# An attention and expert kernel on one core: routing steps on VectorE alone, decayed keys and x on GpSimd, one product for both halves, and first weights every second unit

## The chip, the cores and the metric

The kernel runs on one NeuronCore of a Trainium2 chip. The core has five engines with instruction streams of their own: PE (TensorE, matrix products), DVE (VectorE, elementwise work and small reductions), ACT (ScalarE, activation functions and copies), POOL (GpSimd, elementwise work and indirect transfers) and SP (SyncE, transfers). They share the on-chip memory SBUF; PE writes its results to PSUM, which has eight banks of 128 x 512 numbers of four bytes. The metric is the device time of the core in microseconds, the median of several executions. The results must agree with the reference below.

## The reference

Two stages. The first is a gated linear attention, given as a recurrence over the sequence: batch 4, heads 8, length S = 768, head dimension D = 40. The second is a mixture of experts over the resulting rows: 4 x 768 = 3072 tokens of 320 numbers, eight experts, two of them for each token.

```python
for t in range(S):
    m_new = np.maximum(f_gate[:, :, t] + m, i_gate[:, :, t])
    f_stab = np.exp(f_gate[:, :, t] + m - m_new)
    i_stab = np.exp(i_gate[:, :, t] - m_new)
    m = m_new
    C = f_stab * C + i_stab * einsum('bhd,bhe->bhde', vt, kt)
    n = f_stab * n + i_stab * kt
    h_tilde = einsum('bhde,bhe->bhd', C, qt)
    denom = np.maximum(np.abs(einsum('bhd,bhd->bh', n, qt)), 1.0)
    y[:, :, t] = sigmoid(o_gate[:, :, t]) * h_tilde / denom
...
x = y.transpose(0, 2, 1, 3).reshape(3072, 320)
logits = x @ w_gate + np.log1p(np.exp(x @ w_noise)) * noise
top2, top2_w = two largest of 8, softmax over the two
for e in range(8):
    for k in range(2):
        mask = top2[:, k] == e
        h = np.maximum(x[mask] @ w1[e], 0.0)          # 320 -> 1024
        out[mask] += top2_w[mask, k, None] * (h @ w2[e])   # 1024 -> 320
```

## The kernel before, in words

**Attention by units.** The sequence is cut into 12 chunks of L = 64 positions, and the four batches into two pairs. A unit is one chunk of one pair, 128 tokens; there are NU = 24, units 0 to 11 for the first pair and 12 to 23 for the second. The loop `while i < NU` works on three units at once. For unit i it does the state update `c_part` (decayed keys KD times values, by PE; ScalarE copies the state into the next unit's values), the outputs `o_part` (products P times values, into the one bank "o") and `f_part` on DVE, which forms the denominator `dn`, the quotient `tm` and x, `xr = tm * sigmoid(gate)`. For unit i+1 it makes the decayed keys (`k_part`) and the products (`p_part`: scores times weights W, for both halves p = 0, 1 of the partitions, which are the two batches of a pair). For unit i+2 it makes the gate exponents `e_part` (PE, then Exp on ScalarE into W) and the scores `s_part`. It transposes x of unit i-1 (`t_part`) and multiplies the transposed x of unit i-2 by the gate's weights (`l_part`), which gives the router's logits. In the first chunk of a pair there is nothing before it to add, and the last chunk makes no update.

**Routing by groups.** Four units make a group; when the logits of a group are there, `route` starts a generator `g_part`. Its steps are given out between the instructions of the unit loop by `fill(n)`: `f1` of them at the unit's start and one after each of the first denominator steps, `f2` at its end, as the table `RATE` says. A step that must wait for ScalarE or PE yields "wait" and ends the filling. The steps are: softplus of the noise logits (`na`, `t1`, `co`, `ln`, with Exp and Ln issued on ScalarE by `act`), noise and sum (`nl`), the two largest (`mx`, `mi`), a mask `m` and its running sum `base`; then PE is asked for ranks (a request in the list `want`, served by `r_part`); from the ranks follow each token's slot `ix`, its parts `ai` and `bi`, and the one-hot tiles OA (128 x 448, then multiplied by a sign column) and OB (two of 128 x 512). The list `bursts` then asks PE for eight matmuls of these tiles (`b_part`), whose result is added to the slot table TBL. There is one OA and one OB for all groups. For groups below PG = 4 the softplus steps and the sign product run on POOL, for the others on DVE.

**Experts.** When the first four groups are in the table, four tiles of the first expert's tokens are gathered (`gather(0, 0)`) from the rows that `keep_rows` has written to HBM. From then on the eight experts run one after another: `mm1` (320 to 1024), `mm2` (1024 to 320) and an indirect add into the output. All matrix products there are made of high and low parts in three products.

**What sets the order.** Every engine runs its instructions in the order in which the program issues them; nothing is rescheduled. So an instruction that waits holds back all that stands behind it on its engine, transfers that the engine issues among them. PSUM is given out as eight named banks: one "e", four for scores ("s0" and "s1", two each), one "st" for the state, one "xt" for transposes, logits, ranks and bursts, one "o". SP loads the units' inputs three units ahead, and from unit 6 on pieces of the first expert's first weights, one a unit; `split_w1` then makes the high part on ScalarE and the low part (`w1l`) on POOL, one piece a unit from unit 8 to 13. POOL also writes x to HBM (`keep_rows`) up to unit 11, moves the gates of the units ahead (`gate_move`, every second unit up to 13), and from unit 14 on makes xr itself (XAT = 14). The order within a unit is, for DVE: `k_part(i + 1)`, routing steps, the denominators with routing steps between them, tm and xr, `p_part(i + 1)`, routing steps.

Of the kernel before, what the change touches and what calls it, by code (L numbers as in the profile page):

```python
# [18 lines left out]
L = 64  # L19
# [14 lines left out]

PG = 4
# [3 lines left out]
RATE = ((10, (1, 3)), (14, (3, 4)), (18, (4, 6)), (NU, (6, 9)))  # L39

XAT = 14
# [7 lines left out]
XV = 13  # L49
GC = 2  # L50
# [3 lines left out]
W1LD, W1AT, W2AT = 6, 8, 14  # L54
# [10 lines left out]
def build(ctx, tc, qk, vk, fi, noise, wgn, w1, w2, cst, ce, out):  # L65
# [203 lines left out]
    SP.dma_start(cs[:, C_TRI:], cst[:, C_TRI:])  # L269
    SP.dma_start(wgt, wgn)  # L270
    SP.dma_start(nzt, noise)
# [16 lines left out]
    for j in range(2):  # L288
        for p in range(2):
            psum.tile([128, 512], F32, name=f"s{p}", bufs=2)  # L290
# [29 lines left out]
    def s_room(u):  # L320
        SQ[u] = [psum.tile([128, 512], F32, name=f"s{p}", bufs=2).rearrange("p (h t) -> p h t", h=H) for p in range(2)]

    def s_part(u):
        q = QK[u % 4]
        if whole(u):

            for p in range(2):
                r = qrow[p]
                T.matmul(SQ[u][p][r], ident[r, r], q[r, 0], start=True, stop=True)
        for h in range(H):  # L330
            for p in range(2):
                r = qrow[p]
                T.matmul(SQ[u][p][half[p], h, :], q[r, 1, h, :], q[r, 0, h, :], start=True, stop=True)  # L333
# [4 lines left out]
    def k_part(u):  # L338
        if u % NCH < NCH - 1:
            KD[u] = wk.tile([128, 2, H, D], F32, name="kd")  # L340
            V.tensor_mul(KD[u], VKS[u % 4][:, :, 328:648].rearrange("p x (h d) -> p x h d", h=H),
                         W[u][:, :, :, L - 1:L].to_broadcast([128, 2, H, D]))

    def p_part(u):
        w = W[u]
        PP[u] = [wk.tile([128, H, L], F32, name=f"p{p}") for p in range(2)]
        for p in range(2):
            n = kr(u, p) if whole(u) else half[p]
            V.tensor_mul(PP[u][p][n], SQ[u][p][n], w[n, p])  # L349
# [14 lines left out]
    def o_part(u):  # L364
        for h in range(H):
            for p in range(2):
                n = kr(u, p)
                T.matmul(OQ[u][half[p], h, :], PP[u][p][n, h, :], VK[u % 4][p][n, h * 41:h * 41 + 41], start=True, stop=True)  # L368

    def f_part(u, step):  # L370
# [11 lines left out]
        (P if u >= XAT else V).tensor_mul(XR[u], tm.rearrange("p h d -> p (h d)"), SG[u % 4])  # L382
# [24 lines left out]
    def l_part(i):  # L407

        t = XTB if i < NU else psum.tile([128, 512], F32, name="e")
# [17 lines left out]
    def b_part(t):  # L427

        b = bursts.pop(0) if bursts else None
# [48 lines left out]
    def g_part(g):  # L478
# [7 lines left out]
        Q = P if g < PG else V  # L486
        na = sm("na", [128, nb, NE])
        if Q is P:
            P.tensor_scalar(na, s, 0.0, 2.0, op0=OP.max, op1=OP.mult)
            P.tensor_sub(na, s, na)  # L490
        else:
            V.scalar_tensor_tensor(na, s, -1.0, s, op0=OP.mult, op1=OP.min)
# [6 lines left out]
        Q.tensor_scalar(t1, ue, 1.0, None, op0=OP.add)  # L499
# [8 lines left out]
        Q.tensor_mul(co, co, na)  # L508
# [3 lines left out]
        Q.tensor_sub(ln, ln, co)  # L512
        yield
        if Q is P:
            P.tensor_scalar(na, s, 0.0, None, op0=OP.max)
            P.tensor_add(ln, ln, na)
        else:
            V.scalar_tensor_tensor(ln, s, 0.0, ln, op0=OP.max, op1=OP.add)
        yield
        Q.tensor_mul(ln, ln, nzt[:, u0:u0 + nb, :])  # L520
        yield
        nl = sm("nl", [128, nb, NE])
        Q.tensor_add(nl, ln, lg[:, :, 0:8])
# [36 lines left out]
        asked = [m[:, :, 1:], base[:, :, 0:nb], base[:, :, nb], rk, False]  # L560
# [43 lines left out]
        while busy and not (done[0] >= u0):  # L604
# [6 lines left out]
        (P if g < PG else V).tensor_mul(OA[:, 0:n], OA[:, 0:n].bitcast(F32),  # L611
                                        cs[:, C_SGN + 2 * u0:C_SGN + 2 * u0 + n, None].to_broadcast([128, n, C]))
# [5 lines left out]
        bursts.append((OBS(n), OAS(n)))  # L618
# [60 lines left out]
    turn = dict(h=0, x=0, y=0)  # L679

    def bank(use):

        n = dict(h=("s0", "s1", "e"), x=("s0", "s1"), y=("st", "o"))[use]
        turn[use] += 1
        name = n[turn[use] % len(n)]
        return psum.tile([128, 512], F32, name=name, bufs=2 if name in ("s0", "s1") else 1)
# [66 lines left out]
    begun = 0  # L753
    clear = zeros()
    pre1 = split_w1(P)
    i = 0
    while i < NU:
        f1, f2 = at(RATE, i)
        while sent:
# [3 lines left out]
        if i:  # L763
            keep_rows(i - 1)
        if i % 2 == 0 and i and i // 2 + 2 < 2 * GB:
            gate_move(i // 2 + 2, (P, P) if i < XV else (SP, SP))

        if W1LD <= i < W1LD + 6:
            piece_w1(0, 512 * ((i - W1LD) // 3), (i - W1LD) % 3)
        if W2AT <= i < W2AT + 4:  # L770
            early_w2(2 * (i - W2AT), 2)
        if i == 3:
            constants()
# [4 lines left out]
        if i + 1 < NU:  # L778
            k_part(i + 1)
        if i + 2 == NU:  # L780
            p_part(i + 1)
        if i == 0:
            sig_part(0)
        if i == 6:
            V.tensor_copy(tri, cs[:, C_TRI:C_TRI + 128])
            V.tensor_copy(ones, cs[:, C_ONE:C_ONE + 128])
        fill(f1)
# [8 lines left out]
        if i + 2 < NU:  # L796
            p_part(i + 1)
# [29 lines left out]
        if W1AT <= i < W1AT + 6:  # L827
# [341 lines left out]
```

## Time and profile before

| | us |
|---|---|
| median of 3 runs | 596.63 |
| lowest and highest run | 592.9, 598.4 |
| the profiled execution, its own time | 597.4 |
| its span from the first to the last instruction | 595.5 |
| start and units 0 to 2 | 0 to 40.5 |
| units 3 to 5 | 40.5 to 54.5 |
| units 6 to 21 | 54.5 to 161.5 |
| units 22, 23, last logits | 161.5 to 175.1 |
| experts | 175.1 to 595.5 |

A unit is counted here from the start of its outputs on PE (`o_part`, line 368) to the next one's. Rows of the trace give the start and the length in microseconds, the engine, the line, the operation, the output and inputs with their shape, and in brackets the idle time of the engine just before, with what ended it. A row in which several instructions are taken together ends in their count (x8). Granted clock 1.00 means that PE ran at full speed, 0.50 at half.

### The profile page before, as it was taken

How to read it: one execution, taken by the hardware profiler on the slowest of the kernel's cores; microseconds unless marked ns; L12 is line 12 of the kernel's file. 1: busy time of each engine (PE TensorE's matmuls, PEld its weight loads, DVE VectorE, ACT ScalarE, POOL GpSimd, SP SyncE). 2: the span in 40 equal slices, each digit the busy share in tenths (PEclk: the TensorE clock that was granted, in tenths of full speed). 3: DMA queues.
4: the chain of work that ended last, by engine and by line, in shares of the span. 5: the costliest groups of instructions: out<-in, count | busy, mean ns of one | idle time of the engine just before them, and what ended most of it. 6: DMA issues, size and time to landing. Idle time of an engine off the chain costs nothing.

```text
span 595.5 us, 13323 instructions
## 1 busy us (share of the span) xinstructions
PE 556.7 (93%) x5158; PEld 509.3 (86%) x5158; DVE 353.6 (59%) x958; ACT 255.5 (43%) x621; POOL 229.7 (39%) x308
## 2 busy tenths in 40 slices
PE   7679879999966999999999999999999999999995
PEld 3568767798865889899899989989999998998995
DVE  8589775877867627665466366456546635644611
ACT  6556745575642225452253155135225415423500
POOL 8133445424322446604623441470452245142043
PEclk9789867697877999999999999999999999999998
DMA  5868875568313965626443533642544253232024
GB/s 141 200 179 218 230 148 149 158 176 218 84 58 101 334 192 73 183 89 145 69 122 76 92 85 98 148 93 88 136 68 119 55 132 80 89 42 32 2 28 48
DMA packets 40918, 71.10 MB, mean 119 GB/s; under 512 B 8746, under 2 KB 30207, under 8 KB 40849
## 3 DMA queue, kind: packets, MB, share of 16 engines
q1 hardware_dynamic: 29488, 51.20, 30.0%
q0 software_dynamic: 11360, 18.98, 18.4%
q8 instruction: 43, 0.70, 0.5%
q14 instruction: 27, 0.21, 0.1%
HBM read 52.73 MB, written 17.73 MB: 118 GB/s over the span
## 4 chain that ended last, share of the span: by engine, by line
PE 76%; DVE 9%; issue 4%; POOL 3%; DMA 3%; ACT 1%; SPq 1%; another core or an unknown queue 1%; POOLq 0%; DVEq 0%
PE s L877 21%; PE e L877 10%; PE st L896 5%; PE st L895 5%; PE st L897 5%; PE o L896 4%; PE o L895 4%; PE o L897 4%; PE s L746 3%; DMA re<-hl 2%; PE s L333 2%; PE o L368 2%; PE st L359 1%; DVE p L349 1%; PE e L308 1%
## 5 line engine op out<-in xcount | busy, mean ns | idle before, releaser
L921 POOL DMA_INDIRECT y_out<-y,tok x56 | 87.3, 1558 | 217.5 <-DVE y L911 216.7
L877 PE MATMUL s<-xh,w1h 128*128 128x512 f32 (+1 forms) x255 | 76.8, 357 | 0.9 <-DVE xh L750 0.9
L748 ACT ACTIVATE xh<-s 128x384 fp32r<-128x384 f32 (+1 forms) x56 | 25.6, 470 | 105.5 <-PE s L746 105.1
L883 DVE SCALAR_TENSOR_TENSOR hlo<-s,hh 128x512 fp32r<-128x512 f32 (+1 forms) x85 | 47.4, 559 | 37.4 <-ACT hh L882 33.5
L716 POOL DMA_INDIRECT xg<-rows,tok x56 | 57.3, 1022 | 26.1 <-issue 12.2
L877 PE MATMUL s<-xh,w1l 128*128 128x512 f32 (+1 forms) x255 | 62.2, 353 | 0.0
L882 ACT ACTIVATE hh<-s 128x512 fp32r<-128x512 f32 (+1 forms) x85 | 41.9, 492 | 45.0 <-PE s L877 35.2
L895 PE MATMUL st<-w2h,hh 128*128 128x320 f32 x184 | 58.2, 316 | 0.0
L896 PE MATMUL st<-w2l,hh 128*128 128x320 f32 x184 | 57.3, 311 | 0.0
L897 PE MATMUL st<-w2h,hlo 128*128 128x320 f32 x184 | 56.9, 309 | 0.0
L895 PE MATMUL o<-w2h,hh 128*128 128x320 f32 x168 | 53.2, 317 | 0.0
L896 PE MATMUL o<-w2l,hh 128*128 128x320 f32 x168 | 52.3, 312 | 0.0
L897 PE MATMUL o<-w2h,hlo 128*128 128x320 f32 x168 | 52.0, 310 | 0.0
L877 PEld LDWEIGHTS s<-xh,w1h 128*128 128x128 f32 x255 | 46.3, 190 | 6.3 <-ACT xh L748 1.0
L877 PEld LDWEIGHTS s<-xh,w1l 128*128 128x128 f32 x255 | 44.8, 189 | 5.3
L877 PE MATMUL s<-xl,w1h 128*128 128x512 f32 (+1 forms) x170 | 46.2, 353 | 0.5 <-DVE xl L749 0.5
L333 PE MATMUL s<-qk 64*64 64x64 f32 x768 | 41.1, 255 | 0.2
L333 PEld LDWEIGHTS s<-qk 64*64 64x64 f32 x768 | 35.6, 164 | 3.6 <-issue 1.4
L877 PE MATMUL e<-xh,w1h 128*128 128x320 f32 (+1 forms) x129 | 38.5, 352 | 0.0
L749 DVE TENSOR_TENSOR xl<-s,xh 128x256 fp32r<-128x256 f32 (+1 forms) x56 | 22.6, 404 | 24.0 <-ACT xh L748 23.8
L368 PE MATMUL o<-vk,p 104*64 104x41 f32 (+2 forms) x768 | 31.5, 244 | 5.6 <-DVE t L499 3.9
L311 ACT ACTIVATE w<-e 128x512 f32<-128x512 f32 x46 | 27.6, 601 | 20.3 <-PE e L308 20.3
(212 smaller groups left out, 1350.8 us busy)
## 6 DMA issues: line engine op xcount, KB each, us to landing
vk<-vk_in SPq DMA_DIRECT2D x48, 242.0 KB
raw<-w_in SPq DMA_DIRECT2D x7, 1280.0 KB
qk<-qk_in SPq DMA_DIRECT2D x48, 160.0 KB
raw<-w_in SPq DMA_DIRECT2D x7, 1024.0 KB
y_out<-zrow SPq DMA_DIRECT2D x15, 320.0 KB
raw<-w_in SPq DMA_DIRECT2D x18, 256.0 KB
rows<-xr POOLq DMA_DIRECT2D x12, 160.0 KB
rows<-xr SPq DMA_DIRECT2D x12, 160.0 KB
```

Of the source, the lines that this page charges most:

```text
L311: A.activation(W[u][:, p].rearrange("p h t -> p (h t)"), ps, AF.Exp)
L333: T.matmul(SQ[u][p][half[p], h, :], q[r, 1, h, :], q[r, 0, h, :], start=True, stop=True)
L368: T.matmul(OQ[u][half[p], h, :], PP[u][p][n, h, :], VK[u % 4][p][n, h * 41:h * 41 + 41], start=True, stop=True)
L716: P.indirect_dma_start(out=XG[0:rows_of(t), t], out_offset=None, in_=XD[0:n], in_offset=bass.IndirectOffsetOnAxis(ap=token(e, t), axis=0), ...
L748: A.activation(XH[:, :, c], ps[:, :, 0:n], AF.Copy)
L877: T.matmul(ps[:, 0:n], l, r, start=i == 0, stop=i == len(ops) - 1)
L882: A.activation(HH[:, f, c], ps[:, 0:m], AF.Relu)
L883: V.scalar_tensor_tensor(HLO[:, f, c], ps[:, 0:m], 0.0, HH[:, f, c].bitcast(F32), op0=OP.max, op1=OP.subtract)
L895: T.matmul(ps, HH[:, j, c], W2H[:, j], start=j == 0, stop=False)
L896: T.matmul(ps, HH[:, j, c], W2L[:, j], start=False, stop=False)
L897: T.matmul(ps, HLO[:, j, c], W2H[:, j], start=False, stop=j == 7)
L921: st = P.indirect_dma_start(out=out, out_offset=bass.IndirectOffsetOnAxis(ap=token(e, t), axis=0), in_=y[0:n], in_offset=None, compute_op= ...
```

## The change

The names of new and moved parts, in the order of the diff:

- **k_part and xr:** both products run on POOL, the decayed keys from unit 2 on (KP), xr always. `k_part(i + 1)` is issued directly behind `keep_rows(i - 1)`, ahead of `gate_move`.
- **p_part:** the scores of both halves are one tile of two banks, and one instruction of 128 x 1024 makes the products, other than in the first chunk of a pair. It is issued at the unit's start, ahead of `fill(f1)` and of the denominators of unit i, not behind them.
- **Routing:** all steps on DVE, some of them in a shorter form; a new RATE; requests for ranks and bursts carry the unit from which PE may serve them: the next unit for groups 0 to 2, the same one for the later groups.
- **Weights and constants:** pieces of first weights are loaded and split every second unit, the low part on DVE; the early second weights are loaded from unit 19 on in place of 14; a part of the constants is loaded at unit 3, the noise at unit 4, and `constants()` runs at unit 6.
- **Experts:** the four first gathers are two at unit 22 and two at unit 23; last logits use the bank "st"; the banks for expert products are halves of the two-bank tile.

On DVE, in unit 10, the part of group 0's routing that makes the one-hot tiles stands in these rows before (dn, tm and xr belong to unit 10, p and kd to unit 11):

```order
L599 TENSOR_SCALAR ai_1362<-ix_1344 128x8
L602 SCALAR_TENSOR_TENSOR bi_1364<-ai_1362,ix_1344 128x8
L608 TENSOR_TENSOR oa<-cs,ai_1362 128x448
L373 TENSOR_SCALAR dn<-o 128x8
L615 TENSOR_TENSOR ob<-cs,bi_1364 128x512
L375 SCALAR_TENSOR_TENSOR dn<-o,dn 128x8
L615 TENSOR_TENSOR ob<-cs,bi_1364 128x512
L377 RECIPROCAL dn<-dn 128x8
L381 TENSOR_TENSOR tm<-o,dn 128x320
L382 TENSOR_TENSOR xr<-tm,vk_104 128x320
L349 TENSOR_TENSOR p_1420<-s_1239,w 104x512
L349 TENSOR_TENSOR p_1421<-s_1240,w 128x512
```

The same place on DVE after the change:

```order
L587 TENSOR_SCALAR ai_1310<-ix_1305 128x8
L342 TENSOR_TENSOR p<-s,w 128x1024
L590 SCALAR_TENSOR_TENSOR bi_1325<-ai_1310,ix_1305 128x8
L596 TENSOR_TENSOR oa<-cs,ai_1310 128x448
L599 TENSOR_TENSOR oa<-oa,cs 128x448
L603 TENSOR_TENSOR ob<-cs,bi_1325 128x512 x2
L370 TENSOR_SCALAR dn<-o 128x8
L372 SCALAR_TENSOR_TENSOR dn<-o,dn 128x8
L484 SCALAR_TENSOR_TENSOR na_1375<-lg 128x32
L374 RECIPROCAL dn<-dn 128x8
L378 TENSOR_TENSOR tm<-o,dn 128x320
```

The product p has moved ahead of the one-hot tiles and the denominators, the sign product stands in the row behind oa, and all four one-hot rows are ahead of the first dn.

On PE, at the end of group 0's routing, before the change, the burst (xt from oa and ob) stands in unit 10, behind that unit's logits (xt from wgt):

```order
L308 MATMUL e<-re_90,le_92 128x512
L413 MATMUL xt<-wgt,xts 128x16 x3
L433 MATMUL xt<-oa,ob 128x56 x8
L393 MATMUL xt<-cs,xr 128x128 x3
L308 MATMUL e<-re_90,le_92 128x512
```

After the change, from unit 10's state update (st from vk and kd) on:

```order
L356 MATMUL st<-vk_104,kd 40x41 x16
L365 MATMUL o<-vk_104,p 64x41 x16
L303 MATMUL e<-re_90,le_92 128x512
L410 MATMUL xt<-wgt,xts 128x16 x3
L390 MATMUL xt<-cs,xr 128x128 x3
L303 MATMUL e<-re_90,le_92 128x512
L328 MATMUL s<-qk_98 64x64 x16
L365 MATMUL o<-vk_105,p 64x41 x16
L303 MATMUL e<-re_90,le_92 128x512
L410 MATMUL xt<-wgt,xts 128x16 x3
L430 MATMUL xt<-oa,ob 128x56 x8
```

The burst has moved behind the outputs and logits of unit 11; unit 11, the last chunk of its pair, makes no update (st) ahead of its outputs.

On POOL, around units 9 and 10, before (rows<-xr is `keep_rows`, le and re are the gates of units ahead):

```order
L385 DMA rows<-xr 128x320
L145 TENSOR_TENSOR w1l<-raw_113,w1h 128x512
L830 MEMSET xg 128x336
L385 DMA rows<-xr 128x320
L220 DMA le_93<-hl 32x2x64
L222 DMA re_91<-hl 1x16x128 x2
L611 TENSOR_TENSOR oa<-oa,cs 128x448
L443 TENSOR_TENSOR tbl<-tbl,share 128x56
L489 TENSOR_SCALAR na_1467<-lg 128x32
```

And after:

```order
L382 DMA rows<-xr 128x320
L336 TENSOR_TENSOR kd<-vk_104,w 128x640
L379 TENSOR_TENSOR xr<-tm,vk_103 128x320
L832 MEMSET xg 128x336
L382 DMA rows<-xr 128x320
L218 DMA le_93<-hl 32x2x64
L220 DMA re_91<-hl 1x16x128 x2
L379 TENSOR_TENSOR xr<-tm,vk_104 128x320
```

In place of the weights' low part, the sign product and the softplus, POOL's queue now holds kd and xr of each unit, kd ahead of the gate transfers and xr behind them; unit 11 needs no kd.

The diff, cut to its core:

```diff
-PG = 4
-RATE = ((10, (1, 3)), (14, (3, 4)), (18, (4, 6)), (NU, (6, 9)))
-XAT = 14
+RATE = ((16, (3, 5)), (NU, (5, 8)))
+KP = 2
-W1LD, W1AT, W2AT = 6, 8, 14
+W1LD, W1AT, W2AT = 6, 8, 19
...
     def s_room(u):
-        SQ[u] = [psum.tile([128, 512], F32, name=f"s{p}", bufs=2).rearrange("p (h t) -> p h t", h=H) for p in range(2)]
+        SQ[u] = psum.tile([128, 2, 512], F32, name="s", bufs=2).rearrange("p x (h t) -> p x h t", h=H)
...
-            V.tensor_mul(KD[u], VKS[u % 4][:, :, 328:648].rearrange("p x (h d) -> p x h d", h=H),
+            (P if u >= KP else V).tensor_mul(KD[u], VKS[u % 4][:, :, 328:648].rearrange("p x (h d) -> p x h d", h=H),
...
     def p_part(u):
+        PP[u] = wk.tile([128, 2, H, L], F32, name="p")
+        if whole(u):
+            V.tensor_mul(PP[u], SQ[u], W[u])
...
-        (P if u >= XAT else V).tensor_mul(XR[u], tm.rearrange("p h d -> p (h d)"), SG[u % 4])
+        P.tensor_mul(XR[u], tm.rearrange("p h d -> p (h d)"), SG[u % 4])
...
-        w = want.pop(0) if want else None
+        w = want.pop(0) if want and want[0][5] <= unit[0] else None
...
-        b = bursts.pop(0) if bursts else None
+        b = bursts.pop(0) if bursts and bursts[0][2] <= unit[0] else None
...
-        asked = [m[:, :, 1:], base[:, :, 0:nb], base[:, :, nb], rk, False]
+        asked = [m[:, :, 1:], base[:, :, 0:nb], base[:, :, nb], rk, False, unit[0] + (g < 3)]
...
-        (P if g < PG else V).tensor_mul(OA[:, 0:n], OA[:, 0:n].bitcast(F32),
+        V.tensor_mul(OA[:, 0:n], OA[:, 0:n].bitcast(F32),
...
-        bursts.append((OBS(n), OAS(n)))
+        bursts.append((OBS(n), OAS(n), unit[0] + (g < 3)))
...
-    pre1 = split_w1(P)
+    pre1 = split_w1(V)
...
         if i:
             keep_rows(i - 1)
+        if i + 1 < NU:
+            k_part(i + 1)
...
-        if W1LD <= i < W1LD + 6:
-            piece_w1(0, 512 * ((i - W1LD) // 3), (i - W1LD) % 3)
+        if W1LD <= i < W1LD + 12 and i % 2 == 0:
...
-            gather(0, 0)
+            begun = 1
+        if begun and late < len(tiles(0, 0)):
+            n = 2 if i + 1 < NU else 4
+            gather(0, 0, tiles(0, 0)[late:late + n])
+            late += n
             begun = 2
...
+        if i + 1 < NU:
+            p_part(i + 1)
         fill(f1)
...
         f_part(i, fill if i + 2 < NU else (lambda: None))
-        if i + 2 < NU:
-            p_part(i + 1)
```

More of the change, by code (lines that the diff above doesn't have):

```diff
@@ L288, in build @@
     for j in range(2):
-        for p in range(2):
-            psum.tile([128, 512], F32, name=f"s{p}", bufs=2)
+        psum.tile([128, 2, 512], F32, name="s", bufs=2)
     psum.tile([128, 512], F32, name="st")
@@ L507, in g_part @@
         yield
-        Q.tensor_mul(co, co, na)
+        V.tensor_mul(co, co, na)
         while acts:
@@ L750, in transpose_x @@
         V.tensor_sub(XH[0:64, 2, c], ps[64:128, 2, 0:n], XH[64:128, 2, c].bitcast(F32))
-    begun = 0
+    begun = late = 0
+    unit = [0]
     clear = zeros()
-    pre1 = split_w1(P)
+    pre1 = split_w1(V)
     i = 0
@@ L758, in build @@
         f1, f2 = at(RATE, i)
+        unit[0] = i
         while sent:
```

65 lines of the change are left out of this document (30 added, 35 removed).

## The prediction

> **What bounds the kernel now.** I read a table of stages first, then TensorE's rows with an idle time in front, then DVE and POOL grouped by line, then the rows around single stalls.
>
> ```profile
> span 595.5 us, 13323 instructions
> ...
> 40.50:54.50 14.00, 14.00 (x344) 12.55 (x338) 12.01 (x32) 11.23 (x27) 3.23 (x6) 1.00 0.63 166
> 54.50:161.50 107.00, 97.45 (x1792) 86.44 (x1788) 80.89 (x270) 65.91 (x169) 46.51 (x84) 0.80 0.66 171
> 161.50:175.10 13.60, 9.07 (x108) 8.38 (x105) 7.79 (x29) 5.45 (x15) 5.56 (x6) 0.72 0.25 76
> 175.10:595.50 420.40, 406.60 (x2493) 381.50 (x2492) 222.49 (x558) 149.98 (x371) 154.19 (x172) 0.99 0.43 100
> ```
>
> The stage rows give window, length, then busy time of PE, PEld, DVE, ACT and POOL, the granted clock, the DMA share and GB/s. From 175.1 us the experts run with PE busy 97% at clock 0.99; nothing in the diff shortens their matmuls. What can move is the attention, three stages of it. Units 3 to 5 (40.5 to 54.5) show what a unit costs undisturbed: PE never idle, full clock, 14.00/3 = 4.67 us. Units 6 to 21 (54.5 to 161.5) do the same work with routing mixed in and take 107.0 us for 16 units, 6.69 each.
>
> Of these 107.0 us PE is idle 107.0 - 97.45 = 9.6. Its need at full clock is 16 x 4.67 = 74.7 plus four bursts at 1.18 (row at 156.71 below) = 4.7, so 79.4. The other 97.45 - 79.4 = 18.0 us are matmuls slowed by a lower clock. A state update in undisturbed units (49.18), the idle places, and the stretches at half clock:
>
> ```profile
> 49.18 0.82 PE L359 MATMUL st<-vk,kd 104*40 104x41 f32 x32
> ...
> 63.17 0.68 PE L308 MATMUL e<-re,le 98*128 98x512 f32 x1 [0.91 <-ACT w L311]
> 82.85 1.91 PE L433 MATMUL xt<-oa,ob 128*128 128x56 f32 x8 [3.56 <-POOL oa L611]
> 102.54 0.28 PE L368 MATMUL o<-vk,p 104*64 104x41 f32 x2 [1.23 <-DVE p L349]
> 114.32 1.75 PE L433 MATMUL xt<-oa,ob 128*128 128x56 f32 x8 [1.08 <-POOL oa L611]
> 138.08 1.58 PE L433 MATMUL xt<-oa,ob 128*128 128x56 f32 x8 [0.95 <-DVE ob L615]
> 156.71 1.18 PE L433 MATMUL xt<-oa,ob 128*128 128x56 f32 x8 [0.52 <-POOL oa L611]
> ...
> 63.30:66.70 3.40, 3.38 (x53) 2.65 (x55) 1.67 (x6) 2.16 (x6) 2.62 (x6) 0.50 1.00 293
> 80.40:97.50 17.10, 14.63 (x187) 13.24 (x187) 8.77 (x19) 7.68 (x20) 9.87 (x19) 0.50 0.84 189
> 104.30:111.10 6.80, 6.44 (x82) 5.50 (x83) 6.53 (x23) 4.29 (x11) 2.28 (x3) 0.50 0.54 146
> 114.50:121.40 6.90, 6.88 (x96) 6.14 (x96) 3.58 (x10) 3.28 (x11) 4.15 (x11) 0.51 0.75 207
> 138.40:145.20 6.80, 6.78 (x97) 6.04 (x98) 3.58 (x11) 3.49 (x11) 3.66 (x10) 0.50 0.78 202
> 158.90:162.30 3.40, 3.39 (x76) 3.16 (x68) 3.15 (x11) 1.87 (x5) 2.28 (x3) 0.50 0.14 48
> ```
>
> Each of the six idles stands just before or in a stretch at clock 0.50; in between, PE runs at full clock. So a wait of 1 us costs about four: the middle idle is (0.95 + 1.08)/2 = 1.0 us, the middle stretch 6.8 us, of which half, 3.4, is lost. **A stall costs 4.4 us.** Four of the six are bursts waiting for the routing's one-hot tiles, the fifth (102.54) stands behind the softplus on POOL, the sixth (63.17) behind ScalarE, which itself waits for POOL:
>
> ```profile
> ACT ue L650 <- POOL na L490: 5.9, 3, 2.3
> DVE mx L528 <- POOL nl L523: 5.7, 2, 3.9
> ```
>
> These are waits in line: who waited, for whom, total, times, longest. Weights and products for the next units stand behind them on ScalarE and VectorE.
>
> **The change part by part.** Rows by line for units 6 to 21 (count, busy total, mean in ns), then the same routing rows on DVE for the fifth group, where they stand there already (180 to 192 us):
>
> ```profile
> L341 DVE TENSOR_TENSOR kd<-vk,w 128x640 f32<-128x640 f32 x15 | 12.2, 811 | 2.9 <-ACT w L311 2.7
> L349 DVE TENSOR_TENSOR p<-s,w 128x512 f32<-128x512 f32 x17 | 11.6, 681 | 0.0
> L615 DVE TENSOR_TENSOR ob<-cs,bi 128x512 fp32r<-128x512 f32 x8 | 8.1, 1044 | 0.0
> L381 DVE TENSOR_TENSOR tm<-o,dn 128x320 f32<-128x320 f32 x16 | 7.9, 492 | 0.6
> L382 DVE TENSOR_TENSOR xr<-tm,vk 128x320 f32<-128x320 f32 x8 | 4.0, 505 | 0.6
> L545 DVE TENSOR_TENSOR m<-oh 128x32 bf16<-128x32 f32 x4 | 2.8, 697 | 0.1
> ...
> L382 POOL TENSOR_TENSOR xr<-tm,vk 128x320 f32<-128x320 f32 x8 | 7.0, 869 | 21.3 <-PE xt L393 7.7 <-DVE tm L381 5.6 <-PE e L308 4.3
> L611 POOL TENSOR_TENSOR oa<-oa,cs 128x448 fp32r<-128x448 f32 x4 | 5.0, 1250 | 5.3 <-DVE oa L608 5.2
> L385 POOL DMA_DIRECT2D rows<-xr x6 | 3.6, 601 | 0.2 <-issue 0.2
> ...
> L615 DVE TENSOR_TENSOR ob<-cs,bi 128x512 fp32r<-128x512 f32 x2 | 1.3, 684 | 0.0
> L611 DVE TENSOR_TENSOR oa<-oa,cs 128x448 fp32r<-128x448 f32 x1 | 0.6, 625 | 0.0
> L545 DVE TENSOR_TENSOR m<-oh 128x32 bf16<-128x32 f32 x1 | 0.3, 252 | 0.1
> L523 DVE TENSOR_TENSOR nl<-ln,lg 128x32 f32<-128x32 f32 x1 | 0.2, 191 | 0.0
> ```
>
> *Decayed keys and x to POOL.* DVE loses 12.2 (kd) and 4.0 (xr). POOL's price for 128x640 is not in the trace: between 1.25 (the 128x448 row) and twice the 320 row, 1.74; I take 1.5, nearer the row of 320, with two inputs of the same kind. POOL then has per unit 0.60 (rows out) + 1.5 + 0.87 = 3.0, plus small fills and gate transfers, under 4.67, and the keys have a whole unit until their matmuls. So PE doesn't wait for them. But x now stands behind the keys in POOL's queue and costs 0.87 for 0.50; its transposes come one unit later, which hides 0.4 us. What POOL takes from DVE is the real price. While POOL runs, DVE rows with both sides in SBUF stretch: m 697 against 252, ob 1044 against 684 ns.
>
> ```profile
> 78.16 1.29 DVE L602 SCALAR_TENSOR_TENSOR bi<-ai,ix 128x8 f32<-128x8 int32 x1
> ...
> 78.17 1.26 POOL L145 TENSOR_TENSOR w1l<-raw,w1h 128x512 fp32r<-128x512 f32 x1 [3.35 <-ACT w1h L144]
> ...
> 123.20 1.28 DVE L349 TENSOR_TENSOR p<-s,w 104x512 f32<-104x512 f32 x2
> ...
> 123.42 0.87 POOL L382 TENSOR_TENSOR xr<-tm,vk 128x320 f32<-128x320 f32 x1 [2.31 <-DVE tm L381]
> ```
>
> A tiny op (bi) lasts exactly as long as the POOL op beside it, while p, which reads PSUM, keeps its 1.28 a pair with POOL at work. [...]
>
> POOL's 46.5 us in the stage are an estimated 33 of arithmetic when DMA issues (3.6 for the rows out, and the gates') and fills are taken off; DVE's stretch is 4 x 0.445 (m) + 8 x 0.36 (ob) and about 2.2 for ai and bi, of which the bi row alone is some 1.1: 6.9, or 0.2 us for each of POOL's. Afterwards POOL has 15 x 1.5 + 16 x 0.87 = 36.4. At 0.2 that is 7, at one for one 36; I take 11, as keys and x come every unit, near the low end because most of DVE's time per unit reads PSUM (p, tm, dn).
>
> *Both halves in one p.* 0.68 for 512 and 0.49 for 320 columns give 1.0 ns a column, so 1.19 for 1024 against 1.28 a pair: 16 x 0.09 = 1.5 off. Issued at the unit's start, p no longer stands behind the denominators and their waits: the kind of stall at 102.54 goes.
>
> *Routing on DVE.* Seven small ops of 0.19 (the last of them is the L523 row) are 1.33, and the sign product 0.625: 1.95 a group, add 4 x 1.95 = 7.8. Hops between POOL and DVE, which made the two waits above, vanish; only Exp and Ln stay on ScalarE. The first weights' low part adds six rows of 128x512 on DVE, at ob's 0.684 each 4.1.
>
> DVE sum: 80.9 - 12.2 - 4.0 - 1.5 + 7.8 + 4.1 - 6.9 + 11 = 79.2 us. It stays below the stage's new length, so DVE sets no pace by itself.
>
> *Due units.* Ranks and bursts of groups 0 to 2 go to PE one unit later, so no burst waits for the one-hot tiles. The wait can move, however: the block oa, oa, ob, ob (0.62 + 0.625 + 2 x 0.68 = 2.6) now stands whole ahead of the denominators, and tm after it frees the bank for the next unit's o. In group 0 the next unit has no c_part in front (the last chunk), so o(11) is due 4.67 us after the scores end, tm at 1.2 (p) + 0.2 (bi) + 2.6 + 1.2 (dn to tm: four small ops and tm's 0.49) = 5.2: a stall of 0.5. In the other three the state update gives up to 0.8 us more (the row at 49.18), so they stall only if POOL stretches ob to its 1.04 mean (+0.7). I take 2.5 stalls of the four.
>
> PE sum for units 6 to 21: 79.4 + 2.5 x 4.4 = 11.0 + 3.0 for rank matmuls and small waits = 93.4, against 107.0: **-13.6**. Bounds: no stall 82.4 (-24.6), four 100.0 (-7.0).
>
> *The start.* Units 0 to 2 lose an xr (0.50) and 0.09 of each p on DVE, ahead of the gate math: -0.5, bounds -4 (DVE is the late one there) and +2 (keys late on POOL).
>
> *The tail, 161.5 to 175.1.* Four gathers run in one unit and DVE waits 4.7 us for o; PE idles 3.95.
>
> ```profile
> 161.52 1.46 PE L368 MATMUL o<-vk,p 128*64 128x41 f32 x32
> ...
> 166.95 0.17 DVE L373 TENSOR_SCALAR dn<-o 128x8 f32<-128x8 f32 x1 [4.72 <-remote]
> ...
> 168.34 1.92 PE L368 MATMUL o<-vk,p 104*64 104x41 f32 x31 [3.95 <-DVE t L499]
> ```
>
> With two gathers in each of two units, the second pair stands ahead of the last x on POOL. The o that DVE waits for ran from 161.52 for 1.46 us, so the wait of 4.7 goes on four microseconds past its work, while POOL issues gathers; half of it may go: -2, bounds -5 (it goes whole) and +3 (the last gathers land later, and the experts start on them).
>
> *Costed at nothing.* First weights every second unit: last split at unit 18, used after 175, the cover is some 25 us. Second weights at units 19 to 22, needed after 175 as well; the last are asked for at about 161.5, 13 us ahead. Constants and noise are loaded at units 3 and 4 and the fills stand at unit 6: the routing that uses them starts after that. Late logits in another bank and the experts' halves of one tile: the same banks in the same turn.
>
> Sum: -13.6 - 0.5 - 2 = -16. The profiled span 595.5 becomes 579.5, its run of 597.4 about 581.4; the median of the runs, 596.63, lies 0.8 below that run, so **581** by the median.
>
> **The rivals.**
>
> *DVE and POOL lock each other, slower.* All 36 us of POOL arithmetic stretch DVE: 79.2 + 25 = 104, and with the waits for PE that DVE has now (about 10) 114 against 107, so +7, no gain at the start, +2 at the tail: about 605. It decides from about one half of POOL's time lost on DVE. For it: the bi row. Against: p, tm and dn read PSUM.
>
> *The wait only moves.* Every group stalls at the block, and ranks or x on POOL add two places: 79.4 + 6 x 4.4 + 3 = 108.8; with five, 104.4. About 592 to 597 with the start and tail. For it: the block ahead of the denominators. Against: deadlines are one unit later.
>
> *PE sets the pace throughout.* No stall at all: 82.4, so -24.6 - 2.5: 570. [...]
>
> **How the numbers follow.** Forecast (575 to 589) 0.51; wait moves (590 to 602) 0.19; PE throughout (566 to 574) 0.16; mutual lock (over 602) 0.14. A measurement of this kernel tells about 1%, 6 us, from no change: faster 0.67, same 0.19, slower 0.14. The range 568 to 598 leaves out the lock case and the ends of its neighbours.
>
> **What would show it.** Units 6 to 21 near 93 us with DVE near 79 busy; bursts without a wait before them, o of unit 11 waiting for tm; clock above 0.85 there; kd on POOL near 1.5. Wrong if DVE rows beside POOL stretch by more than 20 us, if half clock stands where PE had no idle, or if the tail keeps its 3.95.

## The result, and the profile after

The changed kernel takes 660.5 us, the median of 4 runs (656.62 to 661.88); the kernel before, 596.14 (4 runs). The ratio is 1.107, with a 95% interval of 1.100 to 1.114: 11% slower. The forecast was 581, faster.

The stages of the kernel after, by the same marks as before (start of the outputs of unit 3, 6 and 22 on PE, first expert product); the columns are window, length, busy time of PE, PEld, DVE, ACT and POOL, granted clock, DMA share, GB/s:

```profile
span 658.3 us, 13322 instructions
...
37.02:54.41 17.39, 14.90 (x340) 12.90 (x334) 16.56 (x28) 12.63 (x30) 9.90 (x13) 1.00 0.72 191
54.41:156.14 101.73, 90.32 (x1784) 79.85 (x1786) 85.05 (x269) 64.15 (x166) 49.37 (x67) 0.88 0.69 178
156.14:172.16 16.02, 9.43 (x110) 8.02 (x105) 9.68 (x46) 5.33 (x15) 5.45 (x6) 0.80 0.30 84
172.16:658.30 486.14, 426.25 (x2492) 392.14 (x2492) 220.83 (x539) 150.62 (x371) 154.40 (x172) 0.96 0.38 86
```

| stage | before | after | difference |
|---|---|---|---|
| start, units 0 to 2 | 40.5 | 37.0 | -3.5 |
| units 3 to 5 | 14.0 | 17.4 | +3.4 |
| units 6 to 21 | 107.0 | 101.7 | -5.3 |
| tail | 13.6 | 16.0 | +2.4 |
| experts | 420.4 | 486.1 | +65.7 |

The attention, where almost all of the change was made, is 3.0 us shorter. All of the loss is in the experts, whose matmuls the change does not touch: PE runs the same products there, but it stands idle 486.14 - 426.25 = 59.9 us, where it was 13.8 before, and its rows take 19.7 us longer at a granted clock of 0.96 in place of 0.99. The list of PE's waits in that stage, after the change (who waited, for whom, total, times, longest), says for what:

```profile
PE s L879 <- DVE ht L888: 21.5, 17, 2.9
PE s L879 <- DVE hlo L885: 15.2, 10, 4.3
PE s L897 <- DVE hlo L885: 4.6, 1, 4.6
PE s L879 <- DVE xh L744: 4.4, 3, 1.7
PE s L740 <- ACT xh L742: 2.9, 2, 1.5
```

Every waiting row writes to s, the two-bank tile, none to e. Before, the first expert products (line 877 there) waited 1.4 us in all:

```profile
PE s L877 <- DVE xh L750: 0.9, 1, 0.9
PE s L877 <- DVE xl L749: 0.5, 1, 0.5
```

One of the waits, row by row, after the change (start, length, engine, line, what it does, idle time before):

```profile
316.48 0.62 PE L879 MATMUL s<-xh,w1h 128*128 128x512 f32 x2
...
317.61 0.84 PE L879 MATMUL s<-xh,w1l 128*128 128x512 f32 x3
319.92 0.74 PE L879 MATMUL s<-xh,w1h 128*128 128x512 f32 x2 [1.47 <-DVE hlo L885]
...
319.18 0.69 DVE L885 SCALAR_TENSOR_TENSOR hlo<-s,hh 128x512 fp32r<-128x512 f32 x1 [0.72 <-ACT hh L884]
```

The products of one column block go to s from 316.48 to 318.45. The next block, also to s, could start at once in the other half, which is free. It starts at 319.92, right behind the DVE row that reads the block just written (319.18 + 0.69 = 319.87). So writing the second block and reading the first no longer overlap. The program shows that this wait is built in. These are PE's instructions for two blocks that follow each other, as the changed kernel's program has them, with the semaphores that they wait on:

```
L879 MATMUL s<-xh,w1h 128x512 [waits PE_49]
L879 MATMUL s<-xh,w1h 128x512
L879 MATMUL s<-xl,w1h 128x512 x2
L879 MATMUL s<-xh,w1h 128x512
L879 MATMUL s<-xh,w1l 128x512 x3
L879 MATMUL s<-xh,w1h 128x512 [waits DVE_49]
```

The last row begins the second block, in the other half of the same tile, and waits for DVE. In this program all 43 blocks of first expert products that go to the second half of a two-bank tile wait for a DVE row that reads the first half: 38 of them for hlo or ht, one or two blocks back, and 5 for xh. None of the 42 blocks in a first half waits for DVE. In the program of the kernel before, no block in s0 or s1 waits for hlo or ht; 33 of the 43 blocks in e do, and the row they wait for is three blocks back.

### The profile page after: what moved, and what is told of

Its sections match the earlier page's. It is cut to its first block, busy times and chain, and to the rows that moved or that the text cites. A ratio compares the mean times of both kernels' runs of the same rounds, so it can differ in the third digit from the quotient of the medians.

```text
span 658.3 us, 13322 instructions
## 1 busy us (share of the span) xinstructions
PE 571.9 (87%) x5158; PEld 514.8 (78%) x5158; DVE 361.1 (55%) x940; ACT 255.6 (39%) x621; POOL 241.4 (37%) x296
## 3 DMA queue, kind: packets, MB, share of 16 engines
q0 software_dynamic: 11360, 18.98, 17.1%
## 4 chain that ended last, share of the span: by engine, by line
PE 58%; DVE 17%; issue 11%; ACT 7%; DMA 4%; POOL 2%; SPq 0%; POOLq 0%; ACTq 0%; DVEq 0%
PE s L879 15%; PE e L879 6%; DVE hlo L885 4%; PE o L897 4%; PE o L898 4%; PE o L899 4%; PE st L898 3%; PE st L897 3%; PE st L899 3%; ACT hh L884 3%; DMA vk<-vk_in 3%; PE s L740 2%; DVE p L342 2%; PE s L328 2%; PE o L365 2%
## 5 line engine op out<-in xcount | busy, mean ns | idle before, releaser
L879 PE MATMUL s<-xh,w1h 128*128 128x512 f32 (+1 forms) x255 | 81.7, 376 | 43.7 <-DVE ht L888 21.5
L879 PE MATMUL s<-xh,w1l 128*128 128x512 f32 (+1 forms) x255 | 64.8, 364 | 0.0
L879 PEld LDWEIGHTS s<-xh,w1l 128*128 128x128 f32 x255 | 46.6, 197 | 5.7
L879 PE MATMUL s<-xl,w1h 128*128 128x512 f32 (+1 forms) x170 | 47.6, 362 | 0.0
L379 POOL TENSOR_TENSOR xr<-tm,vk 128x320 f32<-128x320 f32 x24 | 20.9, 873 | 65.1 <-ACT w L306 12.6
L143 DVE TENSOR_TENSOR w1l<-raw,w1h 128x512 fp32r<-128x512 f32 (+1 forms) x48 | 35.2, 733 | 15.4 <-ACT w1h L142 13.8
L365 PE MATMUL o<-vk,p 128*64 128x41 f32 (+2 forms) x768 | 29.7, 238 | 11.9 <-DVE tm L378 4.1
L879 PE MATMUL e<-xh,w1h 128*128 128x320 f32 (+1 forms) x129 | 39.9, 364 | 0.0
L328 PE MATMUL s<-qk 64*64 64x64 f32 x768 | 38.8, 245 | 0.4 <-DVE hl L209 0.2
```

The source lines that it names most:

```text
L143: lo.tensor_sub(W1L[n, k, s], RAW1[n, k, s], W1H[n, k, s].bitcast(F32))
L328: T.matmul(SQ[u][:, p][half[p], h, :], q[r, 1, h, :], q[r, 0, h, :], start=True, stop=True)
L365: T.matmul(OQ[u][half[p], h, :], PP[u][n, p, h, :], VK[u % 4][p][n, h * 41:h * 41 + 41], start=True, stop=True)
L879: T.matmul(ps[:, 0:n], l, r, start=i == 0, stop=i == len(ops) - 1)
```

## The experiments

The theory after the result: a two-bank tile that is handed out in halves makes the second half wait for the readers of the first, and this is the whole loss. The rivals were too few tiles in turn, and something else that slows the experts (late loads, VectorE's rows). The experiments ran on three chips, four on each, and each chip has its own runs of the kernel before; between chips, ratios to the kernel before are to be compared.

**Single banks for the experts.** The attention keeps its two-bank score tile, but its four banks are given back at unit 23 and taken again as four tiles of one bank:

```diff
+    sp = ExitStack()
+    psc = sp.enter_context(tc.tile_pool(name="psc", bufs=1, space=bass.MemoryType.PSUM))
     for j in range(2):
-        psum.tile([128, 2, 512], F32, name="s", bufs=2)
+        psc.tile([128, 2, 512], F32, name="s", bufs=2)
...
-        n = dict(h=("s", "s", "e"), x=("s", "s"), y=("st", "o"))[use]
+        n = dict(h=("s0", "s1", "e"), x=("s0", "s1"), y=("st", "o"))[use]
...
+        if i + 1 == NU:
+            sp.close()
+            pse = ctx.enter_context(tc.tile_pool(name="pse", bufs=1, space=bass.MemoryType.PSUM, reuse_waits="tile"))
```

> The changed kernel with the experts' products in four tiles of one bank each, as before the change; the attention keeps its two-bank score tile and is unchanged. Theory (shared tile): a product written to one half of a two-bank tile waits for the readers of the other half, and all of the loss is there: the experts take 420 to 424 us again instead of 486, the waits of PE for hlo and ht ahead of the first expert product fall from 37 us to under 3, and the kernel takes 593 to 599 us. Rival (late loads or VectorE rows in the experts' stage): the experts stay above 460 us and the kernel above 635.

Measured: 589.76 us against 597.41, ratio 0.988 (0.981 to 0.995). The experts take 417.4 us, and the waits for hlo and ht are gone. The experts' stage of this kernel, and PE's longest waits in it:

```profile
169.90:587.30 417.40, 406.60 (x2492) 382.26 (x2492) 219.68 (x539) 149.30 (x371) 153.48 (x172) 0.99 0.44 100
...
PE o L421 <- DVE tbl L439: 2.7, 1, 2.7
PE s L881 <- DVE xh L743: 0.9, 1, 0.9
PE s L881 <- DVE xl L742: 0.5, 1, 0.5
```

PE's busy time, 406.60, is that of the kernel before to a tenth. This edit alone turns the 660.5 us of the changed kernel into 589.8, below the range that was expected.

**One half only.** The experts use the first half of each two-bank tile, so there are fewer banks in turn, but no two blocks share a tile:

```diff
-        if not halves:
-            t = psum.tile([128, 2, 512], F32, name="s", bufs=2)
-            halves.extend((t[:, 1], t[:, 0]))
-        return halves.pop()
+        return psum.tile([128, 2, 512], F32, name="s", bufs=2)[:, 0]
```

> The changed kernel, in which the experts use only the first half of each two-bank tile, so that there are two banks of s and one e instead of four and one. Theory (shared tile): no two steps share a tile, so PE's waits for hlo and ht in the experts fall below half of the 37 us of the changed kernel, and the time is 595 to 630 us. Rival (too few tiles in turn): with fewer banks the waits grow, and the time is 665 us or more.

Measured: 595.13 us, ratio 0.997 (0.993 to 1.001); the experts take 423.8 us, and PE's waits for hlo are 3.9 us in one place, those for ht are gone:

```profile
168.75:592.50 423.75, 408.47 (x2492) 381.53 (x2492) 220.50 (x540) 149.75 (x371) 153.76 (x172) 0.99 0.43 99
...
PE s L875 <- DVE hlo L881: 3.9, 1, 3.9
```

Half of the banks, left unused, are better than all of them in shared tiles. So it is not the number of banks, but what a wait is tied to.

**The tiles alone, in the kernel before.** Nothing of the change but the two-bank tile and its halves:

```diff
-        SQ[u] = [psum.tile([128, 512], F32, name=f"s{p}", bufs=2).rearrange("p (h t) -> p h t", h=H) for p in range(2)]
+        sq = psum.tile([128, 2, 512], F32, name="s", bufs=2)
+        SQ[u] = [sq[:, p].rearrange("p (h t) -> p h t", h=H) for p in range(2)]
...
+        if not halves:
+            t = psum.tile([128, 2, 512], F32, name="s", bufs=2)
+            halves.extend((t[:, 1], t[:, 0]))
+        return halves.pop()
```

> The kernel before with nothing changed but the tiles: scores and expert products in halves of two-bank tiles; p stays two instructions of 512 columns. Theory (shared tile): the experts take about 480 to 490 us, and the kernel 655 to 670. In the attention a little more, since p of one half may wait for the scores of both. Rival (something else in the change costs the experts the time): within 1% of 596 us.

Measured: 659.54 us (2 runs), ratio 1.104 (1.091 to 1.117), with the same waits in the experts:

```profile
171.55:653.80 482.25, 422.34 (x2492) 388.63 (x2492) 220.93 (x538) 150.99 (x370) 154.17 (x172) 0.97 0.38 87
...
PE s L883 <- DVE ht L892: 21.6, 17, 2.9
PE s L883 <- DVE hlo L889: 10.9, 9, 1.5
```

The edit to the tiles alone brings the whole loss into the kernel before, and taking it out of the changed kernel takes the whole loss away. Its cause is shown in both directions.

**Decayed keys back on DVE,** in the kernel with single banks:

```diff
-            (P if u >= KP else V).tensor_mul(KD[u], VKS[u % 4][:, :, 328:648].rearrange("p x (h d) -> p x h d", h=H),
+            V.tensor_mul(KD[u], VKS[u % 4][:, :, 328:648].rearrange("p x (h d) -> p x h d", h=H),
```

> The first kernel of this call (single banks for the experts), with the decayed keys back on VectorE. Theory (lock): POOL's keys take more of VectorE's time than they save, since VectorE rows with both sides in SBUF wait for POOL's 1.3 us row in every unit; with the keys back, units 3 to 5 return from 17.4 us to 14 to 15.5, and the kernel is 3 to 8 us faster than the first. Rival (VectorE is relieved): units 6 to 21 grow from 101.7 us to over 107, and the kernel is 4 us or more slower than the first.

Measured: 585.13 us, against 589.76 of the kernel with the keys on POOL on the same chip; the ranges do not touch (584.56 to 586.74, and 589.1 to 591.42). Units 3 to 5 and 6 to 21, first with the keys on POOL, then with them on DVE:

```profile
36.81:54.19 17.38, 14.92 (x334) 12.91 (x334) 16.55 (x28) 11.58 (x27) 9.89 (x13) 1.00 0.73 191
54.19:155.98 101.79, 90.32 (x1786) 79.97 (x1786) 85.25 (x269) 64.16 (x166) 49.36 (x67) 0.88 0.68 178
```

```profile
36.39:50.35 13.96, 13.96 (x343) 12.50 (x339) 13.16 (x30) 11.48 (x28) 5.34 (x9) 1.00 0.84 226
50.35:150.70 100.35, 91.11 (x1794) 81.37 (x1790) 85.45 (x277) 64.76 (x169) 29.57 (x50) 0.86 0.69 180
```

The third busy time is DVE's. In units 6 to 21 it is 85.25 us without the keys and 85.45 with them: 15 rows that took 13.3 us on DVE left it, and it gained nothing. The two windows cut the units at slightly different rows (one product p more without the keys); over the whole attention DVE is busy 140.8 us without the keys (0 to 170 us) and 137.9 with them (0 to 166), so the finding stands. In units 3 to 5 it is 3.4 us more busy without them. Where this went, in the changed kernel, DVE then POOL:

```profile
37.29 0.77 DVE L193 TENSOR_TENSOR xg<-raw,xg 64x128 f32<-64x128 f32 x1
38.10 0.28 DVE L195 TENSOR_TENSOR xg<-xg 64x128 f32<-64x128 f32 x1
38.41 2.01 DVE L200 TENSOR_TENSOR_SCAN xg<-raw,xg 64x128 f32<-64x128 f32 x1
...
37.02 0.89 POOL L379 TENSOR_TENSOR xr<-tm,vk 128x320 f32<-128x320 f32 x1 [0.18 <-DVE tm L378]
...
38.83 1.30 POOL L336 TENSOR_TENSOR kd<-vk,w 128x640 f32<-128x640 f32 x1
```

The scan of 64 x 128 (L200, 0.42 us in the kernel before, median of three) lasts 2.01, until 0.3 us after the keys on POOL are done (38.83 + 1.30 = 40.13); the first row, 0.28 us in the kernel before, ends 0.15 us behind x on POOL (37.91).

**x back on DVE,** up to unit 13, in the kernel with the keys on DVE:

```diff
-        P.tensor_mul(XR[u], tm.rearrange("p h d -> p (h d)"), SG[u % 4])
+        (P if u >= 14 else V).tensor_mul(XR[u], tm.rearrange("p h d -> p (h d)"), SG[u % 4])
```

> The fastest kernel so far (single banks for the experts, decayed keys on VectorE), with x on VectorE up to unit 13, as before the change. Theory (lock): x on POOL for 14 units saves VectorE 14 x 0.5 = 7 us and takes back about as much by rows that wait for its 0.87 us, as the keys did; the time stays within 3 us of 585. Rival (x on POOL pays): VectorE's busy time in units 6 to 21 grows by 4 us and the kernel by 4 us or more.

Measured: 581.64 us (579.58 to 587.22), ratio 0.9785 (0.973 to 0.984), where the kernel with the keys alone put back had 0.9802. No difference that the intervals can tell. DVE's busy time in units 6 to 21 is 83.8 us with these eight rows more on it, and was 85.45 without; over the whole attention it is 137.3 (0 to 167 us) against 137.9. In these profiles (this one is of the slowest of the five runs) x on POOL relieved it of nothing either.

**Ranks and bursts in the unit that asks for them,** for all groups:

```diff
-        bursts.append((OBS(n), OAS(n), unit[0] + (g < 3)))
+        bursts.append((OBS(n), OAS(n), unit[0]))
```

and the same for the ranks.

> The fastest kernel so far (585), with ranks and bursts of all groups served in the unit that asks for them. Theory (bursts wait for the one-hot tiles, each wait brings half clock): three bursts wait 1 us or more on PE again, and units 6 to 21 grow from 100 us by 4 to 10 us: 589 to 595. Rival (the delay only moves the wait): within 2 us of 585.

Measured: 584.35 us, ratio 0.983 (0.978 to 0.988): the same as with the delay. The bursts do wait again, by 3.08, 3.17, 1.45 and 0.46 us on PE:

```profile
77.25 1.91 PE L432 MATMUL xt<-oa,ob 128*128 128x56 f32 x8 [3.08 <-DVE ob L605]
...
103.03 1.91 PE L432 MATMUL xt<-oa,ob 128*128 128x56 f32 x8 [3.17 <-DVE ob L605]
127.24 1.91 PE L432 MATMUL xt<-oa,ob 128*128 128x56 f32 x8 [1.45 <-DVE ob L605]
...
146.79 1.23 PE L432 MATMUL xt<-oa,ob 128*128 128x56 f32 x8 [0.46 <-DVE ob L605]
```

With the delay, in the kernel with the keys on DVE, PE waits in the neighbouring units for the outputs instead, at units 11, 15 and 19:

```profile
78.17 1.13 PE L367 MATMUL o<-vk,p 104*64 104x41 f32 x32 [3.15 <-issue]
...
103.18 1.81 PE L367 MATMUL o<-vk,p 104*64 104x41 f32 x32 [2.27 <-DVE t L493]
...
130.05 1.44 PE L367 MATMUL o<-vk,p 104*64 104x41 f32 x32 [1.57 <-DVE t L493]
```

Four waits of 8.2 us in all against three of 7.0: the delay mostly moves the wait. At unit 11, ahead of the row at 78.17, DVE runs the one-hot block and then tm, of the same kernel:

```profile
75.13 0.62 DVE L601 TENSOR_TENSOR oa<-oa,cs 128x448 fp32r<-128x448 f32 x1
75.67 1.29 DVE L605 TENSOR_TENSOR ob<-cs,bi 128x512 fp32r<-128x512 f32 x2
...
77.58 0.49 DVE L380 TENSOR_TENSOR tm<-o,dn 128x320 f32<-128x320 f32 x1
```

The row that the profile puts down to no releaser starts 0.1 us after tm ends (78.07): PE waits for the same block of rows on DVE, by one way or the other.

**p behind the denominators again,** still one instruction:

```diff
-        if i + 1 < NU:
+        if i + 2 == NU:
             p_part(i + 1)
         fill(f1)
...
         f_part(i, fill if i + 2 < NU else (lambda: None))
+        if i + 2 < NU:
+            p_part(i + 1)
```

> The fastest kernel so far (585), with p issued behind the denominators of the unit, as before the change, as one instruction still. Theory (p no longer waits for denominators): p comes late where routing steps or a wait stand ahead of it, PE's outputs wait for p at several places, and the kernel takes 588 to 595 us. Rival (the early p makes the denominators and tm late instead): the waits of PE for tm and t vanish, and the kernel is as fast or faster, 580 to 586.

Measured: 580.04 us (576.29 to 583.97), ratio 0.975 (0.968 to 0.983), the lowest median of the study, and against the expectation of the theory. The first expert product starts at 160.59 us, 4.6 earlier than with p at the unit's start (165.14). The time is that of the rival, by which p ahead of the denominators keeps tm, and with it the bank of o, back. Its mechanism is seen in part only: PE's waits for the outputs of units 11, 15 and 19 are there still, shorter at the first two:

```profile
79.31 1.13 PE L367 MATMUL o<-vk,p 104*64 104x41 f32 x32 [2.26 <-issue]
...
103.92 1.71 PE L367 MATMUL o<-vk,p 104*64 104x41 f32 x32 [1.89 <-DVE t L493]
...
130.33 1.13 PE L367 MATMUL o<-vk,p 104*64 104x41 f32 x32 [1.57 <-DVE t L493]
```

They were 3.15, 2.27 and 1.57. Between the two profiles, the time up to unit 6 is 3.9 us longer with the late p, units 6 to 21 are 5.3 shorter and the tail 3.2 shorter, which these waits do not account for. The two intervals of the ratios (0.973 to 0.987 with the early p) overlap, so a gain is likely and not shown.

**Softplus and sign product on POOL again:**

```diff
+        Q = P if g < 4 else V
...
-        V.tensor_scalar(t1, ue, 1.0, None, op0=OP.add)
+        Q.tensor_scalar(t1, ue, 1.0, None, op0=OP.add)
```

and so for the other steps.

> The fastest kernel so far (585), with the softplus steps and the sign product of groups 0 to 3 on POOL as before the change. Theory (hops): VectorE saves 4 x 1.95 = 8 us of its own, but it waits for POOL in these steps and its rows beside POOL's stretch; PE's outputs wait longer, and the kernel takes 587 to 596 us. Rival (VectorE is relieved): 580 to 584.

Measured: 585.78 us, ratio 0.986 (0.981 to 0.991). Neither side of the expectation: routing on DVE alone changes the time by less than can be told.

**Keys, x and the place of p put back together,** and from this kernel three single steps: four gathers in one unit; the first weights in six units in a row with the low part on POOL; scores in single banks and p in two instructions.

```diff
-            n = 2 if i + 1 < NU else 4
+            n = 4
```

```diff
-    pre1 = split_w1(V)
+    pre1 = split_w1(P)
...
-        if W1LD <= i < W1LD + 12 and i % 2 == 0:
-            j = (i - W1LD) // 2
+        if W1LD <= i < W1LD + 6:
+            j = i - W1LD
...
-        if W1AT <= i < W1AT + 12 and i % 2 == 0:
+        if W1AT <= i < W1AT + 6:
```

```diff
-        if whole(u):
-            V.tensor_mul(PP[u], SQ[u], W[u])
...
+        for p in range(2):
+            n = kr(u, p) if whole(u) else half[p]
+            V.tensor_mul(PP[u][n, p], SQ[u][p][n], W[u][n, p])
```

> Single banks for the experts, and keys, x and the place of p as before the change, together. If the gains of x (3.5 us) and of p's place (5.1 us) add up, 585.1 - 8.6 = 576.5; theory (each takes VectorE's time or delays the denominators): 573 to 579. Rival (they remove the same waits): 579 to 582.

> The first kernel of this call with the four first gathers in one unit, as before the change. Theory of the prediction (the gathers hold back the end of the attention): units 22 and 23 take 2 us longer or more and the kernel is 1 to 4 us slower than the first. Rival (the wait before was chance, or the split delays the experts): within 1 us of the first or faster.

> The first kernel of this call with the first weights loaded and split in six units in a row and their low part on POOL, as before the change. Theory (POOL's 1.3 us rows stretch VectorE's and the splits crowd the first units of the routing): units 6 to 21 grow by 2 to 5 us. Rival (six rows of 0.69 off VectorE help): the same or up to 3 us faster.

> The first kernel of this call with scores in four tiles of one bank through the whole program and p in two instructions, as before the change; no two-bank tile is left. Theory (the joint p saves only 0.07 us a unit, 1.28 - 1.21): within 2 us of the first kernel. Rival (the joint p is what shortens the attention): 3 us slower or more.

On this chip the kernel before takes 593.08 us.

| kernel | us | ratio to before, 95% interval |
|---|---|---|
| the three put back | 581.60 | 0.979 (0.972 to 0.987) |
| and four gathers in one unit | 583.49 | 0.985 (0.977 to 0.993) |
| and first weights as before, on POOL | 581.48 | 0.980 (0.972 to 0.987) |
| and single banks, p in two | 583.99 | 0.987 (0.978 to 0.996) |

The gains of the earlier runs don't add: 581.6 where 576.5 was the sum. Of the three steps none is told from the kernel they start from: the medians differ from 581.6 by +1.9, -0.1 and +2.4 us, and the intervals overlap. The first weights were expected to make units 6 to 21 longer by 2 to 5 us, and the time of the kernel did not change. With four gathers in one unit, the time from unit 22's outputs to the first expert product is 9.7 us in the profile (149.82 to 159.49) against 11.2 with two in each of two (152.18 to 163.37), where a tail at least 2 us longer with four was expected. Which steps give the kernel its 2% over the one before stays open; no step that was taken back alone changed the time by more than about 1%. The last of the four has no two-bank tile at all, and since it needs no separate pool of single banks, it is the simplest of them.

## Why the prediction was wrong

**The step that failed** is in the list costed at nothing: "the experts' halves of one tile: the same banks in the same turn". It is the same memory, but not the same turn: the second half of each pair waits for the readers of the first, in all 43 blocks. Priced at zero, it measured +65.7 us in the changed kernel and +61.9 by itself in the kernel before (482.25 against 420.4). The waits stand in the changed kernel's instructions (the last row of that listing), apart from any timing; but the places that the prediction weighed are all in the attention, since the experts' matmuls were the same. The stage held 420 of 595 us with PE busy 97%, where a wait has nothing to hide behind.

With this term taken out, the kernel with single banks measures 589.8 where 581 was forecast: the sign was right, and half of the size. In its profile the span is 8.2 us below that of the kernel before, where 16 were forecast, and 3.0 of the 8.2 lie in the experts (420.4 to 417.4), for which nothing was forecast. That the sign came out is partly luck. Its steps, from that kernel's profile:

- *Units 6 to 21, -13.6 forecast, -5.2 measured (107.0 to 101.8).* Three of the four bursts stopped waiting, as forecast, but in place of 2.5 stalls there were ten waits of 0.3 to 2.75 us: for tm, for routing steps on DVE, for the weights W. "The wait only moves", the rival with 0.19, is what happened in this stage, though its price of 104.4 to 108.8 was not reached. The place that was worked out, unit 11, shows how; rows of the changed kernel on PE (the scores of unit 11), on DVE, and then PE's outputs of unit 11:

```profile
76.08 0.90 PE L328 MATMUL s<-qk 64*64 64x64 f32 x16
...
78.47 0.88 DVE L579 TENSOR_SCALAR ov<-r 128x8 f32<-128x8 f32 x1
...
79.86 1.22 DVE L342 TENSOR_TENSOR p<-s,w 128x1024 f32<-128x1024 f32 x1
...
84.17 0.49 DVE L378 TENSOR_TENSOR tm<-o,dn 128x320 f32<-128x320 f32 x1
...
84.77 1.94 PE L365 MATMUL o<-vk,p 104*64 104x41 f32 x32 [2.75 <-issue]
```

  From p to the end of tm are 84.66 - 79.86 = 4.8 us, where the prediction counted 5.2; but PE was ready at 84.77 - 2.75 = 82.02. The block had about the right length, but the prediction let p begin when the scores are done, at 76.08 + 0.90 = 76.98. It began 2.9 us later, behind tm of unit 9 and routing steps that stand ahead of p on DVE, among them ov, which took 0.88. A stall of 0.5 became 2.75.
- *DVE, 79.2 us busy forecast, 85.3 measured.* POOL's share was undersized. I took 11 us from POOL's 36; the keys alone took back all of the 13 us that they saved. Short SBUF rows became longer on average (ov 790, t 759, co 707 ns, where the shortest of each in the changed kernel takes 171, 170 and 192; with the keys back on DVE the means are 559, 570 and 430). The rival of mutual locking had this stretch, whose cause no run shows, but not its consequence: DVE, at 85 of 102 us, did not become the bound of the stage; in units 3 to 5, at 16.55 of 17.38, it did.
- *Keys on POOL at 1.5 us a row:* 1.30, right to 0.2. *The joint p at 1.19:* 1.21 to 1.22, right to a few hundredths.
- *A stall costs 4.4 us.* Wrong as a rule; see the last section.
- *The tail, -2 forecast:* +0.3 with single banks (13.9), +2.4 in the changed kernel. Splitting the gathers could not be shown to do anything.
- *Start, -0.5 forecast:* -3.7, inside its bounds; no run isolates why. *Units 3 to 5* had no term in the sum: +3.4, which the keys on POOL cost (13.96 us again with them on DVE). Single profiles also vary: the kernel before with two-bank tiles alone, whose attention has the same instructions, took 99.8 us for units 6 to 21 and not 107.0. So a term of a few us read from one profile of this stage is no more exact than that.

## What to carry to other kernels

In both kernels that handed out two-bank PSUM tiles in halves to the experts, PE waited at one half for the readers of the other, and the experts took 65.7 and 61.9 us more. Where parts of a tile are written and read in turn by different engines, make them tiles of their own, as the single banks were (417.4 us in place of 486.1), and give the banks back between stages that want different shapes. When a change alters how storage is cut up, go through every later user of that storage, first in the stage that has no slack, and read the waits of its instructions rather than their number and order. Price a move of work from DVE to POOL with the DVE rows that stand beside it: here 13.3 us moved and none was saved, as rows such as ov (790 ns on average against 559 with the keys on DVE) grew longer.

## What the runs showed of the hardware

The granted clock did not fall at every idle of about 1 us, as the six places of the kernel before had made me believe. In the changed kernel PE waits about as long ahead of the outputs of several units, and they still run at full clock, 1.13 us for 32 matmuls; the first stage row above has 1.00 through units 3 to 5:

```profile
42.79 1.13 PE L365 MATMUL o<-vk,p 104*64 104x41 f32 x32 [0.88 <-DVE tm L378]
48.52 1.13 PE L365 MATMUL o<-vk,p 104*64 104x41 f32 x32 [0.53 <-DVE tm L378]
54.41 1.13 PE L365 MATMUL o<-vk,p 104*64 104x41 f32 x32 [1.00 <-DVE tm L378]
...
78.15 1.13 PE L365 MATMUL o<-vk,p 104*64 104x41 f32 x32 [0.43 <-DVE tm L378]
```

The row at 84.77, shown above, takes 1.94 us where the others take 1.13. PE is idle there from 82.02 on, and the granted clock is 1.00 from 80.5 to 83.9 us and 0.50 from 83.9 to 94.1. The half-clock stretches that the prediction lists show one thing that it did not read from them: they start 0, 5, 12, 15, 22 and 28 times 3.41 us behind the first (63.3, 80.4, 104.3, 114.5, 138.4, 158.9), and they last 1, 5, 2, 2, 2 and 1 times as long. In that execution all changes of the clock lie whole multiples of 3.41 us apart. The half-clock stretches beside the six waits lasted 3.4 to 17.1 us, and 4.4 us was the middle of six cases, not a price.

The length of the idle time alone does not tell these cases apart: in the kernel before, 0.52 us of it before the burst at 156.71 stand ahead of half clock from 158.9 on, and in the changed kernel, behind the 1.00 us before the row at 54.41, the clock is 1.00 up to 83.9. What the granted clock goes by, no run shows.

A scan of 64 x 128 on DVE took 2.01 us beside a row transfer's issue (0.60 us) and the keys (1.30) on POOL, where its median in the kernel before is 0.42. And moving 13.3 us of rows off DVE left its busy time where it was, 85.25 against 85.45 us; that DVE's rows beside POOL's would take back all of a move, and not a part, I had not expected.
